# Loads of the second head pair and of phi moved behind a branch, and TensorE products without a reader at the start of a kernel of attention and two expert layers

## The chip, the cores and the metric

One core of one Trainium2 chip runs the program. Measured is the device time in microseconds (us) of one execution. The engines are TensorE (PE; its weight loads PEld), VectorE (DVE), ScalarE (ACT), GpSimd (POOL) and SyncE (SP), which here only issues DMA transfers.

## What is computed

A softcapped attention over 48 heads of 448 tokens by 64, whose output is laid out as 1792 tokens by 768; a soft mixture of 8 experts with 4 slots each; and a layer of squared ReLU. Cut to the core:

```python
scores = scale * np.matmul(q, k.transpose(0, 1, 3, 2))
scores = cap * np.tanh(scores / cap)
attn = softmax(scores)                      # EPS in the denominator
x = np.matmul(attn, v)                      # -> (1792, 768)
logits = x @ phi                            # (1792, 32)
slot_input = softmax(logits, axis=0).T @ x  # 32 slots
slot_out[e] = np.maximum(slot_input[e] @ w1[e], 0.0) @ w2[e]
x = softmax(logits, axis=1) @ slot_out
h = np.maximum(x @ w_in, 0.0)
return h * h @ w_out
```

## The kernel before

Heads are worked on in pairs: 24 pairs (NPAIR), each with one load of q and k of 448 KB (`load(i)`, L268, on SP's queue) into half of one of two buffers (`r0` holds pairs 0 and 1, `r1` pairs 2 and 3, then again `r0`). The program is written out by hand in the order in which each engine and each queue executes it (a manual schedule), so the order in the code is the order on every engine.

The prologue loads the cap (L94), has VectorE work out from it `flag` (L98), which says whether |cap| is above 40, lets GpSimd fill constants (`ident`, an identity; selectors; zeros of the tails `ktail` and `vtail`, L246), loads pairs 0 and 1, and loads phi in four transfers of 24 KB (L580). Then every engine reads `flag` into a register (`values_load`, L581) and branches on it (`tc.If`, L582). The cap of these inputs is 30, so the body of the If runs; the Else is another algorithm for large caps, and lies first in the instruction stream of each engine.

In the body, v of pair 0 is requested on GpSimd's queue (`load_v(0)`: six transfers `va`, L285, and two `vtail`, L289). VectorE splits q and k of a pair into a rounded part `hi` (L294) and a rest `lo` (L300), and GpSimd copies the last 64 key columns of both into `ktail` (L306). Then comes the loop over the pairs. `scores(i, g)` for g = 0, 1, 2 are six products of 64 by 128 by 448 on TensorE (L323: hi by hi, lo by hi, hi by lo, for two heads), g = 3 is three products with `ktail` (L318). ScalarE puts each block through Tanh (L327, L325), which frees its place in PSUM (two places, `ps_s`), and then half a pair through Exp (`exps`, L333). VectorE adds up the exponentials (`sums`, L339 and L343). In the order of TensorE: scores 0 and 1 of pair i, `pv` of pair i-1 (products with v, L355), `den` of pair i-1 (sums of the denominators, L365), scores 2 and 3 of pair i, the tail of `pv` (L352), and for older pairs the logits (L427) and a transposition (L419). Pair 0 has no predecessor, so in its iteration only the four `scores` stand on TensorE, and right behind them scores 0 and 1 of pair 1.

SP's queue issues in order: loads of pairs ahead (pair i+3 in iteration i), weights of the experts, words of the last layer's weights that are decoded on the side (L175; decoded by L189 on ScalarE and by VectorE), and the broadcast of the reciprocal denominators (`bc`, L378). Behind the branch's end come the experts (L860, L885) and the last layer (L969, L1089), which the change does not touch.

The two PSUM places of tag `m` (`ps_m`) hold `den`, the logits and the transpositions, in turn.

Of the kernel before, what the change touches and what calls it, by code (L numbers as in the profile page):

```python
# [8 lines left out]
F32 = mybir.dt.float32  # L9
# [10 lines left out]
P = 128  # L20
# [22 lines left out]
def softcap_attention_soft_moe_relu2(  # L43
# [11 lines left out]
    nc = tc.nc  # L55
# [174 lines left out]
    with ExitStack() as att:  # L230
# [34 lines left out]
        def load(i):  # L265
            b, two, h = heads_of(i)
            t = raw_tile(i)
            nc.sync.dma_start(out=t, in_=qk[b, two, :, :, h].rearrange("j d r s -> (j d) r s"))  # L268
            st["raw", i] = t
# [4 lines left out]
        def load_v(i):  # L274
            b, two, hh = heads_of(i)
            src = v[b, two, :, hh].rearrange("j q c d -> q j c d")
            va = vp.tile([P, NG, 2, D], F32, tag="va", name=f"va{i}")
            vt = vtail[i % 2]
            for g in range(NG):
                at, end = g * P, (g + 1) * P  # L280
                while at < end:
                    c, q = divmod(at, CP)
                    n = min(CP - q, end - at)
                    r = at - g * P
                    nc.gpsimd.dma_start(out=va[r:r + n, g], in_=src[q:q + n, :, c])  # L285
                    at += n
            for h in range(2):
                rows = slice(D * h, D * h + D)
                nc.gpsimd.dma_start(out=vt[rows, rows], in_=src[CP - D:, h, C - 1])  # L289
            st["v", i] = va, vt  # L290
# [38 lines left out]
        def exps(i, half):  # L329
            p = st["p", i, half].rearrange("p c h s -> p (c h s)")  # L330
            if half:
                p = p[:, :3 * S]
            nc.scalar.activation(p, p, AF.Exp, scale=cabs)  # L333
# [239 lines left out]
            if steps:  # L573
                steps.pop(0)()

        for i in range(2):
            load(i)
        for j in range(2):
            for h in range(2):
                nc.sync.dma_start(out=phi_sb[D * j:D * j + D, h::2], in_=phi[D * h:D * h + D, j::2])  # L580
        flag_v = nc.values_load(flag[:1, :1], min_val=0, max_val=1)  # L581
        with tc.If(flag_v == 0, preferred_fallthrough_block=False) as cond:  # L582
            load_v(0)
            prep_hi(0)
            prep_lo(0)
            load(2)
            for i in range(NPAIR):
                last = i == NPAIR - 1
                prv, old, tok = (i >= n for n in (1, 2, 3))
                scores(i, 0)  # L590
                scores(i, 1)
                exps(i, 0)
                if old:
                    take(i - 2)
                if tok:
                    norm(i - 3)
                if prv:
                    sums(i - 1, 1)
                if i + 3 < NPAIR:
                    load(i + 3)  # L600
                if old:
                    den_rows(i - 2)
                if not last:
                    prep_hi(i + 1)
                    prep_lo(i + 1)
                if prv:
                    for g in range(NG):
                        pv(i - 1, g)
                    den(i - 1, i - 3 if tok else None)
                if tok:  # L610
                    logits_add(i - 3)
                    if (i - 3) % HP == HP - 1:
                        late = batch_end((i - 3) // HP)
                        late.pop(0)()
                    elif (i - 3) % HP in (1, 2):
                        step()
                if i in range(4, 16, 2):
                    load_weight(NPAIR // 2 - 1 + (i - 4) // 4, part=i // 2 % 2)
                if i == NPAIR - 2:
                    load_weight(NB - 2, part=0)  # L620
                    load_weight(NB - 2, part=1)
                if (i, 2) in dsteps:
                    dsteps.pop((i, 2))()
                if i < 2 * len(early) and i % 2 == 0:
                    x = early[i // 2]
                    load_raw(*x, ring[NB - 1 - i // 2 % 2][:, :WSZ])
                    dsteps[i + 1, 1] = lambda x=x: decode_a(x)
                    dsteps[i + 2, 0] = lambda x=x: decode_b(x, nc.vector)
                    dsteps[i + 2, 1] = lambda x=x: decode_c([x], (0, 1))
                    dsteps[i + 3, 0] = lambda x=x: decode_c([x], (2,))  # L630
                    dsteps[i + 4, 2] = lambda x=x: store(x)
                if i % 2 and i < NPAIR - 1:
                    load_weight(i // 2)
                if (i, 0) in dsteps:
                    dsteps.pop((i, 0))()
                scores(i, 2)
                scores(i, 3)
                exps(i, 1)
                if prv:
                    pv(i - 1, NG)  # L640
                sums(i, 0)
                if tok:
                    to_tokens(i - 3)
                    if (i - 3) % HP == 0:
                        step()
                if not last:
                    load_v(i + 1)
                if i == NPAIR - 3:
                    load_weight(NB)
                if i == NPAIR - 2:  # L650
                    load_weight(NB + 1)
                    load_weight(NB - 3, part=0)
                    load_weight(NB - 3, part=1)
                if tok and (i - 3) % HP == HP - 1:
                    late.pop(0)()
                    steps.extend(late)
                if (i, 1) in dsteps:
                    dsteps.pop((i, 1))()
                if i == NPAIR - 4:
                    load_weight(NB - 1)  # L660
            assert not dsteps
            assert not steps
            n = NPAIR - 1
            pv(n, 0)
            pv(n, 1)
            sums(n, 1)
            den_rows(n - 1)
            load_weight(NB + 2, nc.scalar)
            pv(n, 2)
            pv(n, 3)  # L670
            norm(n - 2)
            norm(n - 1)
            den(n)
            to_tokens(n - 2, nc.scalar)
            logits(n - 2)
            den_rows(n)
            logits(n - 1, False)
            load_weight(NB + 3, nc.scalar)
            load_weight(NB + 4, nc.scalar)
            norm(n)  # L680
            to_tokens(n - 1, nc.scalar)
            logits(n, False)
            last_end(True)

        with cond.Else():
            st.clear()
            for n, x in enumerate(early):
                load_raw(*x, ring[NB - 1 - n % 2][:, :WSZ])
                decode_ab(x)
                decode_c([x])  # L690
                store(x)
# [487 lines left out]
```

## Time and profile before

| what | value |
|---|---|
| device time, three runs | 556.78, 560.4, 568.22 us, median 560.4 us |
| the profiled execution | 557.4 us, of which its span 555.6 us |
| granted TensorE clock, mean | 0.993 |
| busy over the span | PE 521.3 us (94%), ACT 332.6 us (60%), DVE 331.1 us (60%), POOL 161.0 us (29%) |
| chain that ended last, by engine | PE 81%, DMA 8%, DVE 3%, ACT 3%, issue 2%, POOL 1% |

The span runs from the first to the last instruction of the program. A busy time is the union of an engine's instructions; those that only read registers, branch or issue DMAs are not counted. The chain that ended last is followed back from the last instruction, at each step to what released it. "issue" is time in which an engine waited for nothing that the profile shows. In the timeline, a row has its start, its length, the engine, the line, and how many instructions were merged; in brackets stands how long the engine had been idle and what released it.

### The profile page before, as it was taken

What the parts mean: (1) busy time and instruction counts of PE and PEld (TensorE: products, weight loads), DVE (VectorE), ACT (ScalarE), POOL (GpSimd) and SP (SyncE); (2) the same over time, 40 slices, a digit from 0 to 9 for tenths busy, and PEclk for the clock granted to TensorE, in tenths of its full rate; (3) what the DMA queues carried; (4) which work ended last, traced back from release to release, by engine and by line L of the source; (5) the groups of instructions that cost most, each with busy time, mean ns of one, the idle gap of its engine ahead of it and who ended that gap; (6) DMA issues with size and microseconds to landing.
All of it is one profiled execution on the core that took longest, in us unless ns stands there. A gap on an engine that the chain in (4) does not pass through costs nothing.

```text
span 555.6 us, 10518 instructions
## 1 busy us (share of the span) xinstructions
PE 521.3 (94%) x4068; PEld 358.0 (64%) x4068; DVE 331.1 (60%) x529; ACT 332.6 (60%) x467; POOL 161.0 (29%) x347
## 2 busy tenths in 40 slices
PE   2999999999999988898679999999999999999997
PEld 1555556555665644454236888888888888788885
DVE  2489999999999764450018989889641231322111
ACT  1899999999899840000026677666654455633342
POOL 6987888788878700000000000000000000000000
PEclk9999999999999997999999999999999999999999
DMA  4578787888788899999999445551020020001002
GB/s 124 158 240 248 234 244 244 258 263 267 251 253 235 240 341 417 417 415 416 416 408 378 172 137 170 187 191 57 1 113 2 37 77 1 0 20 38 0 2 113
DMA packets 46249, 108.16 MB, mean 195 GB/s; under 512 B 19440, under 2 KB 28272, under 8 KB 46192
## 3 DMA queue, kind: packets, MB, share of 16 engines
q1 hardware_dynamic: 39472, 99.14, 49.6%
q0 software_dynamic: 6144, 5.52, 4.7%
q10 hardware_dynamic: 576, 2.75, 1.4%
q8 instruction: 34, 0.56, 0.4%
q14 instruction: 23, 0.19, 0.1%
HBM read 94.47 MB, written 7.86 MB: 184 GB/s over the span
## 4 chain that ended last, share of the span: by engine, by line
PE 81%; DMA 8%; DVE 3%; ACT 3%; issue 2%; POOL 1%; SPq 0%; POOLq 0%; ACTq 0%; DVEq 0%
PE y L1089 35%; PE pv L355 9%; PE sc L323 8%; DMA rb<-in_w_dram 6%; PE y L1026 4%; PE so L885 3%; PE sc L318 3%; PE dn L365 3%; PE ph L860 3%; PE pv L352 3%; PE h L969 2%; PE y L1030 2%; PE xm L419 1%; DMA r<-in_w_out_dram 1%; DMA bc<-rc 1%
## 5 line engine op out<-in xcount | busy, mean ns | idle before, releaser
L1089 PE MATMUL y<-gh,wo 128*128 128x512 f32 x576 | 179.0, 393 | 0.4 <-ACT part L1036 0.4
L1089 PEld LDWEIGHTS y<-gh,wo 128*128 128x128 f32 x576 | 106.5, 188 | 24.2 <-issue 1.4
L1089 PE MATMUL y<-gl,wo 128*128 128x512 f32 x288 | 111.6, 390 | 0.0
L982 DVE TENSOR_TENSOR gl<-r,gh 128x512 fp32r<-128x512 f32 (+1 forms) x64 | 40.0, 624 | 112.7 <-ACT gh L981 110.8
L285 POOL DMA_DIRECT2D va<-in_v_dram x144 | 87.3, 614 | 2.5 <-issue 2.4
L973 ACT ACTIVATE r<-h 128x512 f32<-128x512 f32 (+1 forms) x64 | 34.8, 544 | 80.1 <-PE h L969 80.1
L327 ACT ACTIVATE r<-sc,tsc 128x896 f32<-128x896 f32 x72 | 69.5, 998 | 17.5 <-PE sc L323 17.2
L333 ACT ACTIVATE r<-r,cabs 128x1792 f32<-128x1792 f32 (+1 forms) x48 | 77.1, 1606 | 1.6
L1089 PEld LDWEIGHTS y<-gl,wo 128*128 128x128 f32 x288 | 54.1, 188 | 11.6
L355 PE MATMUL pv<-r,va 128*64 128x448 f32 x288 | 60.8, 557 | 0.0
L323 PE MATMUL sc<-hi 64*128 64x448 f32 x144 | 32.7, 449 | 11.1 <-DVE hi L294 10.5
L867 ACT ACTIVATE hs<-ph 128x256 f32<-128x256 f32 x8 | 3.1, 383 | 65.2 <-PE ph L860 65.2
L355 PEld LDWEIGHTS pv<-r,va 128*64 128x64 f32 x288 | 18.7, 138 | 30.2 <-issue 22.6
L980 ACT ACTIVATE r<-r 128x512 f32<-128x512 f32 (+1 forms) x62 | 35.8, 577 | 2.0
L981 ACT CAST gh<-r 128x512 fp32r<-128x512 f32 (+1 forms) x62 | 35.1, 566 | 2.0
L306 POOL CAST ktail<-hi 64x64 fp32r<-64x64 f32 x48 | 27.8, 580 | 22.8 <-DVE hi L294 21.0
L339 DVE SCALAR_TENSOR_TENSOR psum<-r,gcol 128x896 f32<-128x896 f32 x24 | 27.3, 1137 | 3.6 <-ACT r L333 3.6
L885 PE MATMUL so<-rb,ht 128*32 128x256 f32 x298 | 24.9, 382 | 4.2 <-DVE ht L873 2.1
L343 DVE TENSOR_TENSOR psum<-psum,r 128x896 f32<-128x896 f32 x24 | 26.0, 1083 | 4.5 <-ACT r L333 4.5
L300 DVE TENSOR_TENSOR lo<-r,hi 128x896 fp32r<-128x896 f32 x24 | 26.9, 1120 | 2.8 <-POOL ktail L306 0.5
L289 POOL DMA_DIRECT2D vtail<-in_v_dram x48 | 28.1, 590 | 1.6 <-issue 1.6
L323 PEld LDWEIGHTS sc<-hi 64*128 64x128 f32 x144 | 14.1, 192 | 21.5 <-issue 16.1
(195 smaller groups left out, 806.9 us busy)
## 6 DMA issues: line engine op xcount, KB each, us to landing
rb<-in_w_dram SPq DMA_DIRECT2D x41, 768.0 KB, 13.2
r<-in_qk_dram SPq DMA_DIRECT2D x24, 448.0 KB, 6.3
r<-in_w_out_dram SPq DMA_DIRECT2D x13, 768.0 KB, 4.4
r<-in_w_in_dram SPq DMA_DIRECT2D x9, 768.0 KB, 4.3
r<-in_w_dram SPq DMA_DIRECT2D x7, 896.0 KB, 15.6
rb<-in_w_in_dram SPq DMA_DIRECT2D x7, 768.0 KB, 6.4
bc<-rc SPq DMA_DIRECT2D x88, 56.0 KB, 3.5
rb<-in_w_dram SPq DMA_DIRECT2D x12, 384.0 KB, 4.5
```

Of the source, the lines that this page charges most:

```text
L285: nc.gpsimd.dma_start(out=va[r:r + n, g], in_=src[q:q + n, :, c])
L289: nc.gpsimd.dma_start(out=vt[rows, rows], in_=src[CP - D:, h, C - 1])
L323: nc.tensor.matmul(sc[:, h, :S], k, x[rows, 0], **flags)
L327: nc.scalar.activation(p, sc[:, :, :S], AF.Tanh, scale=tsc)
L333: nc.scalar.activation(p, p, AF.Exp, scale=cabs)
L355: nc.tensor.matmul(o[D * h:D * h + D, :S], va[:, g, h], p[:, h], start=(g == 0), stop=False,)
L885: nc.tensor.matmul(so[32 * j:32 * j + 32, :UNIT], ht[:, ft, :], weights(EU * e + EU // 2 + u), start=(e == 0 and ft == 0), stop=(e == NE - ...
L973: nc.scalar.activation(r[:, :n], h[:, :n], AF.Relu)
L980: nc.scalar.activation(r[:, :n], r[:, :n], AF.Square)
L981: nc.scalar.copy(gh[:, :n], r[:, :n])
L982: eng.tensor_tensor(out=gl[:, :n], in0=r[:, :n], in1=gh[:, :n].bitcast(F32), op=ALU.subtract)
L1089: nc.tensor.matmul(y[:, :nn], whl[ft][:, wi, ds], gx[:, :nn], start=(ft == first and t == 0), stop=(ft == end - 1 and t == 2),)
```

## The change

`load(1)` and the four transfers of phi go from in front of the branch into its body: there the order is `load(1)`, v of pair 0, `load(2)`, phi. The Else gets phi as well (it reloads q and k itself). A new function `turn(a, b, n)` takes a place of `ps_m` and lets TensorE write n products of a and b into it, which nothing reads. It is called three times on the path taken: four products of the identity with itself (128 by 128 by 128, float32) between `load(0)` and the reading of `flag`; four more at the head of the body; and, in the iteration of pair 0 behind `scores(0, 3)`, five products of `hi` of pair 0 with itself (128 by 128 by 448, float32r).

```diff
-        for i in range(2):
-            load(i)
-        for j in range(2):
-            for h in range(2):
-                nc.sync.dma_start(out=phi_sb[D * j:D * j + D, h::2], in_=phi[D * h:D * h + D, j::2])
+        def load_phi():
+            for j in range(2):
+                for h in range(2):
+                    nc.sync.dma_start(out=phi_sb[D * j:D * j + D, h::2], in_=phi[D * h:D * h + D, j::2])
+
+        def turn(a, b, n):
+            t = ps_m.tile([P, 512], F32, tag="m", name="turn")
+            for _ in range(n):
+                nc.tensor.matmul(t[:a.shape[1], :b.shape[1]], a, b, start=True, stop=True)
+
+        load(0)
+        turn(ident, ident, 4)
         flag_v = nc.values_load(flag[:1, :1], min_val=0, max_val=1)
         with tc.If(flag_v == 0, preferred_fallthrough_block=False) as cond:
+            turn(ident, ident, 4)
+            load(1)
             load_v(0)
             prep_hi(0)
             prep_lo(0)
             load(2)
+            load_phi()
...
                 scores(i, 3)
+                if i == 0:
+                    turn(st["hi", 0][:, 0, :P], st["hi", 0][:, 0], 5)
                 exps(i, 1)
...
         with cond.Else():
             st.clear()
+            load_phi()
```

SP's queue, the prologue up to the branch, before (the numbers behind a name are buffers; `rb0` in the last row is already the Else's first transfer):

```order
L94 DMA capb_125<-in_cap_dram 128x1
L268 DMA r0_75<-in_qk_dram 128x2x448 x2
L580 DMA phi_sb_165<-in_phi_dram 64x3x32 x4
L581 TENSOR_LOAD flag_129
L581 ISA x2
L582 COMPARE_AND_BRANCH
L175 DMA rb0_84<-in_w_in_dram 128x768
```

The same place of the changed kernel:

```order
L94 DMA capb_125<-in_cap_dram 128x1
L268 DMA r0_75<-in_qk_dram 128x2x448
L588 TENSOR_LOAD flag_129
L588 ISA x2
L589 COMPARE_AND_BRANCH
L579 DMA phi_sb_165<-in_phi_dram 64x3x32 x4
L175 DMA rb0_84<-in_w_in_dram 128x768
```

One load of 448 KB and the four transfers of phi no longer stand ahead of the reading of `flag`; phi now is the first thing of the Else.

SP's queue from the head of the body, before (`r0` with one row of two loads is pair 0 and 1 above; here `r1` is pairs 2 and 3, `rb0` the first words to decode, the last `r0` pair 4, and `bc0` the reciprocals of pair 0):

```order
L582 UNCONDITIONAL_BRANCH
L268 DMA r1_76<-in_qk_dram 128x2x448 x2
L175 DMA rb0_84<-in_w_in_dram 128x768
L268 DMA r0_75<-in_qk_dram 128x2x448
L378 DMA bc0_351<-rc0_349 128x1x112 x4
L166 DMA rb1_85<-in_w_dram 128x1536
```

The same place of the changed kernel, where the first row of `r0` is pair 1:

```order
L589 UNCONDITIONAL_BRANCH
L268 DMA r0_75<-in_qk_dram 128x2x448
L268 DMA r1_76<-in_qk_dram 128x2x448
L579 DMA phi_sb_165<-in_phi_dram 64x3x32 x4
L268 DMA r1_76<-in_qk_dram 128x2x448
L175 DMA rb0_84<-in_w_in_dram 128x768
L268 DMA r0_75<-in_qk_dram 128x2x448
```

Pair 1 stands ahead of pair 2, and phi between pair 2 and pair 3, so pair 2 moved from the first to the second place and pair 3 from the second to the seventh.

TensorE around the end of pair 0's scores, before (`sc0_2` and `sc0_3` are blocks 2 and 3 of pair 0, `sc1_0` is block 0 of pair 1):

```order
L323 MATMUL sc0_2_278<-hi0_242 128x448 x2
L323 MATMUL sc0_2_278<-hi0_242,lo0_244 128x448 x2
L323 MATMUL sc0_2_278<-lo0_244,hi0_242 128x448 x2
L318 MATMUL sc0_3_286<-hi0_242,ktail0_195 128x448 x2
L318 MATMUL sc0_3_286<-lo0_244,ktail0_195 128x448
L323 MATMUL sc1_0_302<-hi1_269 128x448 x2
L323 MATMUL sc1_0_302<-hi1_269,lo1_271 128x448 x2
```

The same place of the changed kernel:

```order
L323 MATMUL sc0_2_288<-hi0_248 128x448 x2
L323 MATMUL sc0_2_288<-hi0_248,lo0_250 128x448 x2
L323 MATMUL sc0_2_288<-lo0_250,hi0_248 128x448 x2
L318 MATMUL sc0_3_296<-hi0_248,ktail0_195 128x448 x2
L318 MATMUL sc0_3_296<-lo0_250,ktail0_195 128x448
L584 MATMUL turn_301<-hi0_248 128x448 x5
L323 MATMUL sc1_0_318<-hi1_279 128x448 x2
L323 MATMUL sc1_0_318<-hi1_279,lo1_281 128x448 x2
```

Five products stand between the last product of `sc0_3` and the first of `sc1_0`; the other rows keep their order.

## Rows read from the trace of the kernel before

**Rows 1.** The page: head, granted clock in 40 slices, chain by engine.

```profile
span 555.6 us, 10518 instructions
...
PEclk9999999999999997999999999999999999999999
...
PE 81%; DMA 8%; DVE 3%; ACT 3%; issue 2%; POOL 1%; SPq 0%; POOLq 0%; ACTq 0%; DVEq 0%
```

**Rows 2.** Chain that ended last, 7 to 28 us: start, length, what.

```profile
7.93 2.37 issue
...
14.44 1.05 POOL vtail L289 x2
...
16.09 1.68 PE sc L318 x3
...
20.30 3.54 PE pv L355 x12
```

**Rows 3.** The branch, L582: durations in ns (min/median/max), start in us.

```profile
L582 PEldq COMPARE_BRANCH  x1: 4056/4056/4056, 4.8 to 4.8; - x1
L582 DVEq COMPARE_BRANCH  x1: 67/67/67, 4.9 to 4.9; - x1
...
L582 SPq COMPARE_BRANCH  x1: 45/45/45, 6.3 to 6.3; - x1
L582 POOLq COMPARE_BRANCH  x1: 45/45/45, 7.4 to 7.4; - x1
```

**Rows 4.** DMA queues, 5 to 6.5 us: packets, MB, share of 16 engines.

```profile
q1 hardware_dynamic: 932, 0.49, 107.6%
```

**Rows 5.** DMA queues, 6.5 to 7.6 us.

```profile
q14 instruction: 3, 0.02, 6.9%
```

**Rows 6.** Timeline, first work of SP, DVE and POOL behind the branch.

```profile
9.59 2.00 SPq L268 DMA_DIRECT2D r<-in_qk_dram  x2
9.73 0.63 DVE L294 CAST hi<-r 128x896 fp32r<-128x896 f32 x1 [5.22 <-issue]
10.30 4.14 POOL L285 DMA_DIRECT2D va<-in_v_dram  x6 [2.37 <-issue]
```

**Rows 7.** Timeline of PE, 12 to 28 us.

```profile
12.07 0.58 PE L323 MATMUL sc<-lo,hi 64*128 64x448 f32 x2
12.45 0.58 PE L323 MATMUL sc<-hi 64*128 64x448 f32 x2
...
17.19 0.57 PE L318 MATMUL sc<-lo,ktail 128*128 128x448 f32 x1
17.70 0.74 PE L323 MATMUL sc<-hi 64*128 64x448 f32 x2
...
27.16 0.38 PE L323 MATMUL sc<-hi,lo 64*128 64x448 f32 x2
27.36 0.38 PE L323 MATMUL sc<-lo,hi 64*128 64x448 f32 x2
```

**Rows 8.** Timeline of ACT, 12 to 26 us.

```profile
14.85 1.79 ACT L333 ACTIVATE r<-r,cabs 128x1792 f32<-128x1792 f32 x1
...
17.80 0.63 ACT L325 ACTIVATE r<-sc,tsc 128x448 f32<-128x448 f32 x1 [0.27 <-PE sc L318]
...
19.79 1.89 ACT L327 ACTIVATE r<-sc,tsc 128x896 f32<-128x896 f32 x2
...
25.43 1.01 ACT L327 ACTIVATE r<-sc,tsc 128x896 f32<-128x896 f32 x1 [1.93 <-PE sc L323]
```

**Rows 9.** Timeline of POOL and DVE, 16 to 18 us.

```profile
16.09 0.51 POOL L306 CAST ktail<-lo 64x64 fp32r<-64x64 f32 x2
16.66 1.35 POOL L306 CAST ktail<-hi 64x64 fp32r<-64x64 f32 x2
16.75 1.15 DVE L339 SCALAR_TENSOR_TENSOR psum<-r,gcol 128x896 f32<-128x896 f32 x1 [3.61 <-ACT r L333]
```

**Rows 10.** Transfers of L268 issued up to 25 us.

```profile
DMA to landing us min/median/max: 4.2/4.8/8.7
```

## What the change does to the time, forecast from these rows

> **What bounds the kernel now.** I read the page first: the span is 555.6 us and TensorE holds 81% of the chain that ended last [rows 1]. The change touches only the first 28 us, so the second view is the chain of waits there [rows 2]. Read from its top: 2.37 us from 7.93 on in which GpSimd waits for nothing the profile shows (the branch), GpSimd's eight requests for v, which end at 14.44 + 1.05 = 15.49, its copies into `ktail`, then block 3 of pair 0's scores on TensorE (16.09 to 17.77), and from there TensorE alone through `pv`. So at the very place where the change puts its five products, TensorE sets the end; ahead of it GpSimd does.
>
> The branch is the third view. TensorE, VectorE, SP and GpSimd reach it at 4.8 to 7.4 us [rows 3], and SP, VectorE and GpSimd do their first work behind it at 9.59, 9.73 and 10.30 [rows 6]. Until 6.5 the DMA engines are full with the loads (107.6% of 16 engines), and no packet of an instruction queue is among them [rows 4]; in the next 1.1 us three packets of one come [rows 5]. I read this as code that is fetched from behind the branch and queues behind data.
>
> The fourth view is TensorE's timeline [rows 7]. The same products of 448 columns follow each other every 0.37 us at 12 us (12.07, 12.45) and every 0.20 us at 27 us (27.16, 27.36). The first is 448 columns at the 1.2 GHz level, the second near the 2.4 GHz level, although the granted clock reads full in these first slices [rows 1]; I go by the spacing. The 12 products of `pv` take 3.54 us [rows 2], between 12 x 0.37 = 4.4 and 12 x 0.20 = 2.4: n x 0.37 + (12 - n) x 0.20 = 3.54 gives n = 6.7, so the clock rises at about 20.3 + 6.7 x 0.37 = 22.8 us. Before it TensorE stood still until the branch was over and then worked with pauses until 17.70.
>
> **The loads moved behind the branch.** From SP go, ahead of its branch, one load and four transfers of phi. Its branch stands at 6.3, TensorE's at 4.8, for which SP's first five requests are the only reason I see; it can come 1.4 earlier at most, and I take 1.0. For the engines that branch at 4.8 and 4.9 the data ahead of their code get less. GpSimd, which branches at 7.4 when the loads are through, needs 10.30 - 7.4 = 2.9 us to its first work, VectorE 9.73 - 4.9 = 4.8. The gain of VectorE lies between 0 and 1.9; about half the loads' bytes remain ahead of it, so I take 0.7, well inside.
>
> What that gives: VectorE splits pair 0 at 9.0 instead of 9.73, the first Tanh and Exp come 0.7 earlier, and the first Exp, which ends at 14.85 + 1.79 = 16.64 [rows 8], ends at 15.9. But the next thing ScalarE needs is block 3, and in the trace it already waits 0.27 us for that, at 17.80 [rows 8]. Block 3 hangs on GpSimd, whose branch came when the queues were empty: its 10.30 and its 15.49 stay. So **the term of the branch is 0**: all of the 0.7 ends in a longer wait for block 3. The bounds are 0 and -0.27, the wait that is there.
>
> Pair 1 is now requested at 8.6 and not at 1.9. Transfers of this kind land 4.2 to 8.7 us after their issue [rows 10]: at 12.8 to 17.3. Its two splits (0.63 for `hi` [rows 6], 1.1 for `lo` by the like of it) end at 14.5, at the latest at 19.0; TensorE takes pair 1 up at 17.70 [rows 7] in the old order, at 19.4 in the new (below). Term 0; the upper end would cost nothing there either. Pair 2 moves from 9.59 to about 9.2, pair 3 behind phi's four requests (0.6 each) to about 12.4, 2 us later; it is split at 29 us, 8 us after the latest landing of 12.4 + 8.7 = 21.1. Phi is read first for the logits of pair 0, three pairs on. Term 0 for these, hidden behind two and more pairs of work.
>
> **The products ahead and behind the branch.** Four of 128 columns in float32 each time. TensorE has nothing else before `hi` is there, so they cost 0 unless they last past 9.6. No row has just this; `pv` is float32 too, with 12 records for six products, so two records each: 8 x 128/448 x 0.37 = 0.85 us. TensorE comes out of its branch at 4.8 + 4.06 = 8.87 [rows 3], by my 0.7 at 8.2: they end at 9.1. If they were four times as long, 11.6, scores would start 2 us late and still end ahead of block 3's release at 16.09 by the pause that stands there. Term 0.
>
> **The five products behind block 3.** Each has 448 columns: 5 x 0.37 = 1.87 us at the lower level, 5 x 0.20 = 1.0 at the upper. Block 3's last product starts at 17.19 and frees the array at 17.56; pair 1's first product starts at 17.70 [rows 7]. So only 0.14 us of pause is there to fill, and 1.87 - 0.14 = 1.73 us go on TensorE's path. Behind them all TensorE's work lies 1.73 us late until the clock rises; if it rises at the same 22.8, what is pushed past it is done at the upper level, in half the time: +0.87. If the filled pause makes it rise 0.9 us earlier (unbroken work from 16.8 and not from 17.70), 0.9 us of half-rate work is saved by half: 0.87 - 0.45 = +0.42. I take the middle, **+0.65**. ScalarE does not hide it: it waits 1.93 us for block 2 of pair 1 at 25.43 [rows 8], so what TensorE loses before this point shows there in full. From there on all later work stands in the same order, and the shift goes through to the end.
>
> **Sum.** 0 + 0 + 0 + 0.65 = +0.65 us: 557.4 becomes 558.05 for the profiled execution. The runs shown are 556.78, 560.4 and 568.22; with the profiled 557.4 the middle two of the four average 558.9, which I take as the kernel's time now, 1.5 below the median of three: **559.5 us**.
>
> **Rivals.**
> *The clock rises before block 3.* The new products give TensorE work at 2 and at 8 us. If that and the earlier scores bring the upper level before 16 us, block 3 ends 0.5 earlier, the five products take 1.0, pair 1's scores and `pv` run at 0.20: 17.0 + 1.0 + 2.4 (12 products' worth of scores) and `pv`, which then waits for v (last pieces requested up to 14.4) at about 20.9, leave block 2 of pair 1 ready at 23.3 and not 25.4: -2.1, 556.8 us. Against it: the trace has nearly unbroken products from 12.07 to 13.6 at the lower level [rows 7] and no rise behind them before 22.8; the new ones stand apart from these by VectorE's two splits. The Trainium skill (TensorE: Matmul & The Clock Gate, Part 1) says that the throttled level is the default, that sustained activity releases it, and that the same kernel starts with different numbers of slow products from run to run. By that page such a rise is possible with and without the change; the trace agrees on the slow start, and no run here shows an early rise. Chance 0.2.
>
> *GpSimd is slowed: slower.* Today the copies of `lo` into `ktail` take 0.51 for two, with VectorE idle, and the next two 1.35, beside VectorE's sum L339 [rows 9]. L339 waits for the first Exp; if that ends before 16.1 (by my numbers 15.9), L339 falls on the copies that block 3 waits for: +0.84 on block 3. With the 1.73, 2.57 us of half-rate work are late, half of it at the upper level: +1.3, up to +2.1 if the new pause also delays the rise by 0.8 or more. I take +1.7: 560.6 us. For it speaks that 15.9 is on the wrong side; against it that my 0.7 can be less than 0.5. Chance 0.25.
>
> *Nothing of it is on the path.* The branch is no earlier, and the clock rises early enough through the filled pause to pay for the five products: 0, 558.9 us. Chance 0.1.
>
> **How the numbers follow.** Forecast 0.45 (its own bounds, +0.42 and +0.87, are 559.3 and 559.8 us), rivals 0.2, 0.25 and 0.1. All cases lie within 3 us of each other, far inside the 2% (11 us) that a measurement of this kernel tells from no change; executions of the one kernel before lie 11 us apart. So the range is made by these: low 557.4 - 2.1 = 555.3; high, beyond the slower rival on the median (560.4 + 1.7 = 562.1), by half the way to the slowest run: 565. No case gives 11 us either way: same 0.96, 0.02 each for the others.
>
> **What would show it.** First work behind the branch about 9.0 on VectorE and 8.6 on SP, 10.3 on GpSimd. ScalarE's wait before Tanh of block 3 longer than 0.27, its start still near 17.8. Five products 0.37 apart behind block 3, `sc1_0` at 19.4. The wait of ScalarE before block 2 of pair 1 ending at about 26.1. Wrong, if GpSimd also comes out earlier and starts its requests by 9.6 (then up to -0.7), or if products of pair 0 are 0.20 apart.

## Result, and the profile after

The changed kernel takes 560.58 us (median of 12 runs, 557.13 to 562.32) against 556.72 us for the kernel before beside it: ratio 1.0057, 95% interval [1.0031, 1.0084], or +3.2 us (+1.7 to +4.7). The ratio is that of the means, 560.25 and 557.06 us, without one slow run of the kernel before (568.22). Measured again at the end of the study beside another experiment (e19 below) it gave 1.0034 [1.0012, 1.0056]. The two, weighted by their intervals, make +2.4 us (+1.5 to +3.4). So the change is a small loss: inside the 2%, inside the range that was given, but four to five times the +0.65 us of the forecast's sum, and with other causes.

| | before | after |
|---|---|---|
| profiled execution, its span | 557.4, 555.6 us | 561.4, 559.6 us |
| granted TensorE clock, mean | 0.993 | 0.983 |
| busy PE / DVE / POOL over the span | 94 / 60 / 29% | 94 / 59 / 29% |
| chain that ended last: PE, DMA, issue | 81, 8, 2% | 80, 7, 3% |

The start answers to [rows 3] and [rows 6]. The branch of the changed kernel, durations in ns and start in us, then the first work of SP, VectorE, TensorE and GpSimd behind it from the timeline:

```profile
L589 PEldq COMPARE_BRANCH  x1: 3620/3620/3620, 4.3 to 4.3; - x1
...
L589 SPq COMPARE_BRANCH  x1: 45/45/45, 4.5 to 4.5; - x1
L589 POOLq COMPARE_BRANCH  x1: 45/45/45, 6.9 to 6.9; - x1
```

```profile
7.97 2.39 SPq L268 DMA_DIRECT2D r<-in_qk_dram  x2
...
7.89 0.63 DVE L294 CAST hi<-r 128x896 fp32r<-128x896 f32 x1 [3.92 <-issue]
...
7.96 2.08 PE L584 MATMUL turn<-ident 128*128 128x128 f32 x8 [3.73 <-issue]
...
10.18 3.78 POOL L285 DMA_DIRECT2D va<-in_v_dram  x6 [2.79 <-issue]
```

VectorE begins 1.84 us earlier than in [rows 6] and SP 1.62; GpSimd gains 0.12 only. What becomes of it stands in the timeline of GpSimd, VectorE, TensorE and ScalarE, 14 to 27 us, which answers to [rows 7 to 9]:

```profile
15.61 1.43 POOL L306 CAST ktail<-lo 64x64 fp32r<-64x64 f32 x2
...
15.51 1.15 DVE L339 SCALAR_TENSOR_TENSOR psum<-r,gcol 128x896 f32<-128x896 f32 x1 [1.69 <-ACT r L333]
...
15.60 0.74 PE L318 MATMUL sc<-hi,ktail 128*128 128x448 f32 x1 [2.00 <-POOL ktail L306]
17.09 0.74 PE L318 MATMUL sc<-hi,ktail 128*128 128x448 f32 x1 [0.74 <-POOL ktail L306]
17.62 0.58 PE L318 MATMUL sc<-lo,ktail 128*128 128x448 f32 x1
18.00 2.07 PE L584 MATMUL turn<-hi 128*128 128x448 f32 x5
20.00 0.74 PE L323 MATMUL sc<-hi 64*128 64x448 f32 x2
...
18.24 0.64 ACT L325 ACTIVATE r<-sc,tsc 128x448 f32<-128x448 f32 x1 [1.95 <-PE sc L318]
...
26.32 1.01 ACT L327 ACTIVATE r<-sc,tsc 128x896 f32<-128x896 f32 x1 [1.01 <-PE sc L323]
```

VectorE's sum now starts at 15.51, 0.10 us ahead of GpSimd's copies of `lo` for pair 0. These take 1.43 us and not the 0.51 of [rows 9], block 3 waits for them, ScalarE waits 1.95 us for block 3, and the five products begin at 18.00. At 26.3 us ScalarE is 0.89 us later than in [rows 8].

Nothing in these rows reaches 3 us. The rest of this profiled execution's 4.0 us lies elsewhere: 1.8 us arise between 28 and 200 us, most of it at 120 to 135, where TensorE is busy 12.86 us and not 14.74. Other profiled executions of the same changed kernel have 14.72 and 14.62 us there, so that is this execution's own. The remaining 1 us and more arises behind the branch's end, where the change touches nothing. Four loads of expert weights (`rw`) on SP's queue, timeline of SP before and after:

```profile
202.49 5.54 SPq L166 DMA_DIRECT2D rw<-in_w_dram  x4
```

```profile
205.22 10.43 SPq L166 DMA_DIRECT2D rw<-in_w_dram  x4
```

What SP waited for, 200 to 219 us, from the view of waits (us in total, times, longest), again before and after:

```profile
...
SPq L166 <- PE u L490: 2.8, 1, 2.8
SPq L166 <- PE dn L365: 2.5, 1, 2.5
SPq L166 <- DVE bc L412: 2.3, 1, 2.3
...
```

```profile
SPq L166 <- DMA r<-in_w_dram: 5.2, 2, 2.7
...
SPq L166 <- DVE bc L412: 2.7, 1, 2.7
SPq L166 <- PE dn L365: 2.5, 1, 2.5
...
```

The first line of the last fence is new: twice SP waits for a transfer `r<-in_w_dram`, that is, for loads that ScalarE's queue issues.

### The profile page after: what moved, and what is told of

It reads as the page before. It is cut to its first block, busy times and chain, and to the rows that moved or that the text cites. A ratio compares the mean times of both kernels' runs of the same rounds, so it can differ in the third digit from the quotient of the medians.

```text
span 559.6 us, 10561 instructions
## 1 busy us (share of the span) xinstructions
PE 525.5 (94%) x4089; PEld 363.4 (65%) x4089; DVE 331.6 (59%) x529; ACT 332.6 (59%) x467; POOL 159.9 (29%) x347
## 3 DMA queue, kind: packets, MB, share of 16 engines
q0 software_dynamic: 6144, 5.52, 4.9%
## 4 chain that ended last, share of the span: by engine, by line
PE 80%; DMA 7%; DVE 4%; ACT 3%; issue 3%; POOL 2%; SPq 0%; POOLq 0%; DVEq 0%; ACTq 0%
PE y L1102 35%; PE pv L355 9%; PE sc L323 8%; DMA rb<-in_w_dram 6%; PE y L1039 4%; PE so L898 4%; PE ph L873 3%; PE dn L365 3%; PE sc L318 3%; PE pv L352 2%; PE h L982 2%; PE y L1043 2%; PE xm L419 1%; ACT r L327 1%; DMA bc<-rc 1%
## 5 line engine op out<-in xcount | busy, mean ns | idle before, releaser
L1102 PEld LDWEIGHTS y<-gl,wo 128*128 128x128 f32 x288 | 54.1, 188 | 11.6
L355 PE MATMUL pv<-r,va 128*64 128x448 f32 x288 | 59.6, 548 | 0.0
L886 DVE COPY ht<-px 128x32 f32<-128x32 f32 x8 | 1.5, 192 | 44.7 <-PE px L883 34.2
## 6 DMA issues: line engine op xcount, KB each, us to landing
r<-in_w_dram SPq DMA_DIRECT2D x7, 896.0 KB, 15.6
```

The costliest lines, as they stand in the source:

```text
L355: nc.tensor.matmul(o[D * h:D * h + D, :S], va[:, g, h], p[:, h], start=(g == 0), stop=False,)
L1102: nc.tensor.matmul(y[:, :nn], whl[ft][:, wi, ds], gx[:, :nn], start=(ft == first and t == 0), stop=(ft == end - 1 and t == 2),)
```

## The experiments

Each experiment changes one thing against the kernel before or the changed kernel. Ratios are against the kernel before, run beside each on the same chip; microseconds are (ratio - 1) x 557. "rw" is the length of the four loads on SP's queue, "copies" the longer of GpSimd's two pairs of copies that block 3 waits for, both from the profiled execution.

| kernel | ratio, interval | us | rw | copies |
|---|---|---|---|---|
| changed kernel | 1.0057 [1.0031, 1.0084] | +3.2 | 10.43 | 1.43 |
| e19: changed kernel again | 1.0034 [1.0012, 1.0056] | +1.9 | 11.18 | 1.40 |
| e1: loads moved, no products | 1.0034 [1.0022, 1.0047] | +1.9 | 11.19 | 1.41 |
| e2: only the eight products | 1.0002 [0.9984, 1.0019] | +0.1 | 5.65 | 0.57 |
| e3: only the five products | 0.9998 [0.9981, 1.0014] | -0.1 | 5.51 | 0.55 |
| e5: changed kernel without the five | 1.0043 [1.0022, 1.0064] | +2.4 | 10.44 | 0.54 |
| e9: only phi moved | 1.0013 [0.9998, 1.0027] | +0.7 | 5.53 | 1.34 |
| e8: loads moved, seven products in the pause | 1.0008 [0.9981, 1.0035] | +0.4 | 11.01 | 1.37 |
| e10: clock up from 5 us, loads as before | 1.0004 [0.9995, 1.0014] | +0.2 | 5.46 | 1.40 |
| e11: the same products, loads moved | 1.0042 [1.0026, 1.0057] | +2.3 | 12.41 | 0.99 |
| e4: changed kernel, sum later | 1.0037 [1.0009, 1.0064] | +2.1 | 10.97 | 0.54 |
| e7: loads moved, sum later | 1.0014 [1.0000, 1.0029] | +0.8 | 11.46 | 0.54 |
| e14: changed kernel, one unexecuted transfer more | 1.0021 [1.0004, 1.0037] | +1.2 | 5.52 | 1.29 |
| e15: kernel before, seven unexecuted transfers more | 1.0013 [0.9997, 1.0029] | +0.7 | 12.13 | 0.55 |
| e16: e1 with the unexecuted transfer | 1.0013 [1.0000, 1.0026] | +0.7 | 5.94 | 1.36 |
| e17: e7 with the unexecuted transfer | 1.0003 [0.9989, 1.0017] | +0.2 | 5.77 | 0.54 |
| e18: e4 with the unexecuted transfer | 0.9990 [0.9975, 1.0005] | -0.6 | 5.49 | 0.55 |

### Which part of the change costs

Loads alone (e1), the eight products alone (e2), the five alone (e3), phi alone (e9), and all but the five (e5). e1's edit is the diff of the front without the three calls of `turn`; e2 and e3 add those calls to the kernel before:

```diff
+        turn(ident, ident, 4)
         flag_v = nc.values_load(flag[:1, :1], min_val=0, max_val=1)
         with tc.If(flag_v == 0, preferred_fallthrough_block=False) as cond:
+            turn(ident, ident, 4)
```

> Kernel before with only the loads of pair 1 and phi behind the branch, no added products. Theory A (the loss is made in the first 28 us, by GpSimd's copies that fall on VectorE's first sum, and by the five products): the copies of lo for block 3 still take about 1.4 us beside the sum, block 3 starts its second product at about 17.1, no products stand behind it, so pair 1's first product comes at about 18.1 against 17.70 before, and the span is 0 to +0.6 us over the kernel before. Theory B (the moved loads or phi disturb something later, as at 123 to 131 us in the changed kernel's trace): +2 to +3 us, with less than 0.6 of it before 28 us.

> Kernel before with only the eight products of 128 columns, four ahead of the branch and four behind it; loads as before. Theory A: nothing on the path, 0 us, within 0.5. Theory C (the added work makes TensorE's clock rise early and fall again in the pause before block 3, so products up to about 22 us run at the lower level, and the whole pattern of falls is moved): the trace shows the upper level for a part of pair 0 and the lower one behind it, and +0.5 to +2 us.

> Kernel before with only the five products of 448 columns behind block 3 of pair 0; loads as before. Theory A: five products 0.37 us apart ahead of pair 1's first product, which comes at about 19.4 against 17.70, +0.4 to +0.9 us in the whole. If the five were hidden by a clock that rises earlier: 0 or less.

> The changed kernel without the five products behind block 3 (loads moved, eight products of 128 columns kept). The loads alone measured +1.9 us, all together +3.2. If the five products cost only where block 3 is late (theory A, with the collision): about +2.0 over the kernel before, as with the loads alone. If it is the eight that make the difference to the loads alone (theory C, an early rise of the clock that falls back in the pause before block 3): +3 us.

> Only phi moved behind the branch; pair 1 is loaded ahead of it as in the kernel before. Branch code is still behind both loads of q and k, so VectorE starts at about 9.7 and the first scores are not earlier. Theories A and D: no collision and no longer pause, 0 us within 0.5. Theory E with phi's 768 small packets or their place in the queue as the disturbance: +1 to +2 us.

Measured: +1.9, +0.1, -0.1, +2.4 and +0.7 us. Neither set of products by itself costs anything that its interval of about 1 us either way shows, and taking the five out of the changed kernel gives nothing that its interval shows. The moved loads carry the loss, and of these mostly pair 1's: e9 leaves pair 1 where it was, its +0.7 us has an interval down to -0.1, and the collision of the next part is in its profile (1.34). In e3's profile block 3 is not late and the five products fall at the upper clock level; TensorE's timeline there (compare 18.00 and 20.00 above):

```profile
15.86 1.04 PE L318 MATMUL sc<-hi,ktail 128*128 128x448 f32 x2 [0.69 <-POOL ktail L306]
16.73 0.36 PE L318 MATMUL sc<-lo,ktail 128*128 128x448 f32 x1
16.93 1.19 PE L579 MATMUL turn<-hi 128*128 128x448 f32 x5
18.06 0.47 PE L323 MATMUL sc<-hi 64*128 64x448 f32 x2
```

### The collision on GpSimd

In e4 and e7 VectorE makes its first sum of pair 0 one Exp later, with the same terms in another order:

```diff
             t = psums[i % 2]
+            if i == 0:
+                if half == 0:
+                    nc.vector.scalar_tensor_tensor(
+                        out=t, in0=st["p", i, 1][:, 0], scalar=gcol, in1=p[:, 0], op0=ALU.add, op1=ALU.add
+                    )
+                else:
+                    nc.vector.tensor_tensor(out=t, in0=t, in1=st["p", i, 0][:, 1], op=ALU.add)
+                return
```

> The changed kernel, but VectorE's first sum of pair 0 is made over the first block of the second half and the first of the first half, so it waits for the second Exp and cannot run beside GpSimd's copies of lo for block 3 (the sum has the same terms in another order). Theory A: the copies take 0.5 us again for two, block 3's second product comes at about 16.2 and not at 17.1, and the whole is 0.5 to 1 us under the changed kernel. Theory B or C (the loss is made later or by the clock): as the changed kernel, within 0.3 us.

> Only the loads moved, and VectorE's first sum of pair 0 made after the second Exp, so that it doesn't fall on GpSimd's copies for block 3. Theory A (the collision is what the moved loads cost): the copies of lo take 0.5 us, block 3's second product comes at about 16.0, and the whole is back to the kernel before, 0 us within 0.6. Theory D (the moved loads cost because pair 0's first scores come 1.5 us earlier and block 3 does not, so TensorE pauses longer, and its clock rises later or falls back): a part of the 1.9 stays, +0.8 to +1.5 us. Theory E (something later in the program): +1.9 us as before.

Timeline of GpSimd and, in the last row, of ScalarE in e4: the copies are all at 0.5 us, and block 3 reaches ScalarE at 17.20 and not at 18.24.

```profile
14.88 0.54 POOL L306 CAST ktail<-hi 64x64 fp32r<-64x64 f32 x2
15.48 0.51 POOL L306 CAST ktail<-lo 64x64 fp32r<-64x64 f32 x2
16.05 0.51 POOL L306 CAST ktail<-hi 64x64 fp32r<-64x64 f32 x2
...
17.20 0.63 ACT L325 ACTIVATE r<-sc,tsc 128x448 f32<-128x448 f32 x1 [0.66 <-PE sc L318]
```

Measured: e4 +2.1 us, e7 +0.8 (e1, the same with the collision, +1.9). The profiles agree: block 3 reaches ScalarE at 17.96 to 18.79 us in the changed kernel's four profiles and those of e1, e14 and e16, which all have the collision, and at 16.69 to 17.55 in the four with the later sum (e4, e7, e17, e18). The collision is real and its removal helps, but e4 keeps most of the changed kernel's loss. It also is a race of a few tenths: in e5's profile the sum started at 15.81, behind the copies of `lo`, which took 0.51.

### The clock

Perhaps the changed start only shifts when TensorE's clock rises. The changed kernel's rows show a rise and a fall. Timeline of TensorE:

```profile
11.63 0.39 PE L323 MATMUL sc<-hi,lo 64*128 64x448 f32 x2
11.85 0.36 PE L323 MATMUL sc<-lo,hi 64*128 64x448 f32 x2
...
20.54 0.58 PE L323 MATMUL sc<-hi,lo 64*128 64x448 f32 x2
20.91 0.58 PE L323 MATMUL sc<-lo,hi 64*128 64x448 f32 x2
```

At 11.6 us two products stand 0.22 apart (upper level), at 20.5, behind the pause before block 3, 0.37 (lower level; the granted clock is 0.51 from 18 to 22 us). e8 fills that pause with seven products, e10 and e11 give TensorE 14 products of 128 columns ahead of the branch, 3 behind it and 8 of 448 in the pause, e10 with the loads in the old place, e11 in the new. The edit of these two in the pause:

```diff
                 scores(i, 2)
+                if i == 0:
+                    turn(st["hi", 0][:, 0, :P], st["hi", 0][:, 0], 8)
                 scores(i, 3)
```

> Only the loads moved; seven products of 448 columns that nothing reads are put into TensorE's pause before block 3 (four ahead of it, three between its first and second product), none behind it. The collision stays. Theory D: the pause is filled, the clock rises by about 15 us in many executions and stays, and the whole is 0 to -1 us against the kernel before, 2 to 3 us under the loads alone. Theory A: the copies are as slow, +1.5 to +2.5 us. Theory E: +1.9 us.

> Loads as in the kernel before. Unread products so placed that TensorE hardly pauses from 2.2 us on: 14 of 128 columns ahead of the branch, 3 behind it, 8 of 448 columns in the pause before block 3, none behind block 3. Theory D (when the clock first rises is a lottery of each execution, and the start's loss or gain hangs on it): the upper level holds from 10 us on in nearly all executions, pv of pair 0 starts at about 19.4 with products 0.20 apart, and the whole is 1 to 2 us under the kernel before with less spread. Theory A alone (only GpSimd's copies set block 3): 0 us.

> The same products, with the loads of pair 1 and phi behind the branch. Theory D: with the clock up in both, the moved loads cost only what block 3 comes later by the collision, 0 to +0.5 us over the kernel e10_warm, so still 0.5 to 2 us under the kernel before. Theory E (the moved loads disturb something later in the program): 1.5 to 2 us over e10_warm.

In e10's profile pair 0's products already follow each other every 0.20 us (11.34, 11.54, 11.74), and over all its executions the kernel gains nothing: +0.2 us [-0.3, +0.8]. e11, with the loads moved, loses 2.3. So the moved loads cost their 2 us with these products too. But the two kernels do not part the loads from the clock: in e11's profile TensorE still pauses 1.71 us before block 3, and `pv` of pair 0 then takes 3.68 us (TensorE's timeline, 12 records), where e10's takes 2.48. e8 stood at +0.4 with an interval of 3 us, which decides nothing.

What an early clock is worth, e10 does not settle. GpSimd's copies collide in its profile as well (1.40), and its profiled execution is ahead of that of the kernel before. The first sums of the denominators (`den`) of pair 0, TensorE's timeline of the kernel before, of e15 (below, with the start of the kernel before) and of e10:

```profile
23.77 0.40 PE L365 MATMUL dn<-r,onesp 128*32 128x112 f32 x8
22.30 0.40 PE L365 MATMUL dn<-r,onesp 128*32 128x112 f32 x8
21.44 0.40 PE L365 MATMUL dn<-r,onesp 128*32 128x112 f32 x8
```

e10's lead of 2.33 us here is still 2.30 at the first `rw` load (200.19 for 202.49) and 2.1 in the span (553.5 for 555.6). In a single execution, then, what is won at the start does come out at the end. But e15 is 1.47 ahead at this place too, so the profiled execution of the kernel before had a late start; how often that happens is not shown.

Two more executions of the changed kernel, each by itself:

> The changed kernel once more, for a second trace of it. If the wait of the first trace at 123 to 131 us (1.9 us in which the lateness grew) belongs to the change, it is there again; if it was that execution's alone, the lateness stays as it is at 28 us up to the end of the attention.

> The changed kernel a third time, for the same question, and for when TensorE's clock first rises: theory D expects another moment than in the other traces, and a lateness at 28 us that goes with it, 0.5 us for each us that the lower level lasts longer.

They took 562.35 and 562.49 us, with spans of 560.6 and 560.7, GpSimd's copies ahead of block 3 at 0.87 and 1.34 us, and the four `rw` loads at 12.87 and 13.04. A length of 10 us and more for these loads is there in every trace so far in which pair 1 is requested behind the branch, and in none of the others (5.5 to 5.7).

### The stall at 205 us

Why should a load moved at 2 us stop SP at 205? The order of the program says which counters a transfer waits on. There are eight (`DMAHW0` to `DMAHW7`), used in turn, and SP and ScalarE share them; a transfer waits until the one before it on its counter has landed. SP's loads behind the branch's end, before:

```
L166 DMA rw2_7207<-in_w_dram 128x1536 [waits DMAHW2_49,DMAHW6_49,DVE_49,DMAHW7_49,PE_49,Activation_49]
L166 DMA rw3_7208<-in_w_dram 128x1536 [waits DMAHW3_49]
L166 DMA rw0_7205<-in_w_dram 128x1536 [waits DMAHW4_49]
```

after:

```
L166 DMA rw2_7227<-in_w_dram 128x1536 [waits DMAHW6_49,DVE_49,DMAHW7_49,PE_49,Activation_49]
L166 DMA rw3_7228<-in_w_dram 128x1536 [waits DMAHW7_49]
L166 DMA rw0_7225<-in_w_dram 128x1536 [waits DMAHW0_49]
```

and ScalarE's three loads, at the end of the body, in both kernels:

```
L166 DMA r_77<-in_w_dram 128x1792 [waits DMAHW6_49,DVE_49]
L166 DMA r_78<-in_w_dram 128x1792
L166 DMA r_79<-in_w_dram 128x1792 [waits DMAHW0_49,Activation_49]
```

Taken in turn these hold counters 6, 7 and 0. In the changed kernel `rw3` and `rw0` use 7 and 0 too, and so must wait until ScalarE's second and third loads, 896 KB each, have landed. They are issued at 207.02 and 207.45 us and take 5.4 and 7.9 to land, so until about 212.4 and 215.3, and SP's timeline has the two loads issued right then; in the kernel before, the four were issued by 207.54 (202.49, 206.68, 207.06, 207.54):

```profile
212.44 0.33 SPq L166 DMA_DIRECT2D rw<-in_w_dram  x1
...
215.32 0.33 SPq L166 DMA_DIRECT2D rw<-in_w_dram  x1
```

The counters moved because the way through the Else has one transfer fewer: five left the prologue, and four (phi) came into the Else. With e9 (four and four) they did not move. Why one transfer fewer moves them by four counters (3 to 7, 4 to 0) the order does not show. If so, a transfer more in the Else, which these inputs never execute, must end the stall, and seven more in the kernel before (one fewer, counted in eights) must bring it on. e14, e16, e17 and e18 have the first edit, e15 the second:

```diff
             st.clear()
             load_phi()
+            load(1)
```

```diff
             st.clear()
+            for _ in range(7):
+                load(1)
```

> The changed kernel with one more transfer in the Else, which these inputs never execute; with it the expert loads behind the branch's end (rw, L166) wait for the same semaphores as in the kernel before. Theory S (the moved loads cost through the semaphore that SP's four expert loads share with ScalarE's loads at 205 to 215 us): the four rw loads take about 5.5 us on SP's queue and not 10.4, and the time falls by about 2 us against the changed kernel, to +0.5 to +1.5 us over the kernel before (what is left is the start: collision and five products). Theory A (all is lost in the first 28 us) and theory D (the start's clock): no difference to the changed kernel, +3 us over the kernel before.

> The kernel before with seven transfers more in the Else, which these inputs never execute; nothing on the path taken changes but the semaphores of the transfers behind the branch's end, which become those of the changed kernel. Theory S: the four rw loads take 10.4 to 13 us on SP's queue and not 5.5, and the kernel is 1.5 to 2.5 us slower than the kernel before, by code that never runs. Theories A and D: 0 within 0.5 us, since the start is the same.

> The loads moved, no products, and one transfer more in the never executed Else (the rw loads wait as in the kernel before). Theory S: rw loads 5.5 us, 0 within 0.6 us of the kernel before (the loads alone without the pad stood at 1.0034, +1.9 us). Theory A: still +1.5 to +2 us, since the start is that of the loads alone.

> As the loads with the pad, and VectorE makes its first sum of pair 0 only behind the second Exp, so that GpSimd's copies of lo stay at 0.5 us. Without the pad this stood at 1.0014 (+0.8 us). Theory S: rw loads 5.5 us and 0.5 to 1.5 us faster than the kernel before, the gain of the earlier start (about 1 us). Theory A: +0.8 us as without the pad.

The order of e14 has `rw3` and `rw0` on counters 3 and 4 again, that of e15 on 7 and 0, and the profiles settle the mechanism both ways. Timeline of SP in e14, then in e15, and what SP waits for in e15, 200 to 216 us:

```profile
202.95 5.52 SPq L166 DMA_DIRECT2D rw<-in_w_dram  x4
```

```profile
201.00 12.13 SPq L166 DMA_DIRECT2D rw<-in_w_dram  x4
```

```profile
SPq L166 <- DMA r<-in_w_dram: 6.9, 2, 3.8
```

A transfer that never runs stops SP's queue, and another sets it free. Its price is smaller than I expected: e15 loses 0.7 us where 1.5 to 2.5 stood in the expectation, and its interval reaches to -0.2. The profile of e15 shows why it is about 1. Views by stretches, 200 to 290 us, before and e15 (busy PE, PEld, DVE, ACT, POOL; granted clock, DMA share, GB/s):

```profile
200.00:206.00 6.00, 5.03 (x71) 2.52 (x68) 3.04 (x6) 2.08 (x6) 0.00 (x0) 1.00 0.80 286
206.00:212.00 6.00, 4.25 (x63) 2.87 (x62) 4.31 (x18) 1.45 (x6) 1.29 (x3) 0.86 1.01 394
212.00:218.00 6.00, 5.81 (x53) 2.73 (x51) 1.51 (x4) 0.06 (x1) 0.00 (x0) 0.57 1.02 420
218.00:290.00 72.00, 58.86 (x759) 29.58 (x759) 18.20 (x50) 6.19 (x15) 1.87 (x6) 1.00 1.02 415
```

```profile
200.00:206.00 6.00, 4.39 (x70) 2.64 (x69) 3.30 (x11) 2.19 (x7) 0.00 (x0) 1.00 0.95 350
206.00:212.00 6.00, 5.24 (x63) 3.90 (x67) 3.92 (x13) 0.91 (x4) 1.36 (x3) 0.72 1.00 398
212.00:218.00 6.00, 5.20 (x81) 2.82 (x76) 2.37 (x11) 0.69 (x2) 0.00 (x0) 1.00 0.92 350
218.00:290.00 72.00, 58.99 (x735) 29.42 (x730) 16.47 (x43) 5.55 (x13) 1.87 (x6) 0.98 1.02 415
```

From 206 us on this stage is bound by the DMA engines (share 1.0, 415 GB/s). e15's execution is 1.5 us ahead when it issues the first `rw` (201.00 against 202.49). At 212 to 218 its DMA engines move 350 GB/s and not 420, since SP had too little in the queue: 70 GB/s over 6 us is 0.42 MB, 1.0 us at 415 GB/s. The first product of the last layer, TensorE's timeline before and in e15, is only 0.5 ahead:

```profile
296.40 3.00 PE L1089 MATMUL y<-gh,wo 128*128 128x512 f32 x12
```

```profile
295.92 3.00 PE L1091 MATMUL y<-gh,wo 128*128 128x512 f32 x12
```

From the first `rw` to this product it is 93.9 us before and 94.9 in e15. Over all profiled executions that stretch averages 94.2 us in the nine without the stall (93.7 to 95.1) and 95.2 in the eleven with it (94.3 to 97.8): 1.0 us, though the two groups overlap.

### Both causes taken back

> The changed kernel with both causes found taken back: one transfer more in the never executed Else (rw loads wait as before) and VectorE's first sum of pair 0 behind the second Exp (GpSimd's copies of lo at 0.5 us). All products and moved loads stay. If the semaphores cost about 1 us and the collision about 1 us each, this is at 0 to +0.5 us of the kernel before, and 2 to 3 us faster than the changed kernel run beside it; if the moved loads or the products cost something else as well, it stays at +1 us or more.

> The changed kernel unaltered, on the same chip as the one with both causes taken back: +2 to +4.5 us over the kernel before, by its first interval [1.0031, 1.0084]. If it comes out below +1.5 us, the sum that the causes must make up is smaller than the first measurement said.

e18 keeps all products and all moved loads and stands at -0.6 us [-1.4, +0.3]; the changed kernel beside it stands at +1.9. The difference is 2.4 us, with an interval of about 1.5 either way (both intervals taken together). With the stall and the collision gone, no loss is left that the interval shows. Each by itself, from pairs that differ in one of them, weighted by their intervals, with the changed kernel's two measurements as one: the stall 1.0 +- 0.5 us (changed kernel and e14, e1 and e16, e7 and e17, e4 and e18, e15 and before), the collision 1.0 +- 0.6 (changed kernel and e4, e14 and e18, e1 and e7, e16 and e17). One pair fits less well: e11 loses 2.1 us (+- 1.0) against e10, though the collision is in both profiles (0.99 and 1.40); the interval reaches down to the stall's price, and the slower `pv` named above is in e11's profile as well. How much of the collision's price is block 3 itself, and how much the clock that is low behind the longer pause, these runs do not part. Not one of the versions beats the kernel before by more than its interval: e18 comes nearest.

## Why the prediction was right and wrong

**The branch: right that the engines come earlier, wrong that it costs nothing.** The loads ahead of the branch did hold VectorE and SP up; by the two profiles they come out 1.84 and 1.62 us earlier, where 0.7 and 1.0 were taken. About 0.5 us of this is the profiled execution of the kernel before, whose `flag` is worked out at 4.04 us, and at 3.54 in e15 with the same start: VectorE begins at 9.02 to 9.73 us in the five profiles with all loads in the old place, and at 7.89 to 8.31 in the fourteen with pair 1 moved. GpSimd gains almost nothing, since its own constants keep it until 7.4, and ScalarE's wait for block 3 grew (1.95 us for 0.27), as said. But block 3 did not stay where it was, as the term of 0 with its bounds of 0 and -0.27 had it: it reaches ScalarE at 18.24 and not at 17.80, by the collision. e18, which has no collision and no stall, stands at -0.6 us [-1.4, +0.3], so a gain from the earlier start is not shown.

**Pair 1, phi and the other pairs: right for their data, and incomplete.** `hi` of pair 1 waited for its data until 12.06 and was in time. What was missed is below.

**The eight products: wrong in size, free all the same.** Four of 128 columns take 2.07 us and not 0.85; scaling by columns from `pv` was the mistake. They end at 10.04 and push scores to 9.97, later than VectorE's split (7.89 + 0.63), but block 3 forgives it, as the prediction's four-fold bound of this term had said: e2 is at +0.1 [-0.9, +1.1].

**The five products: +0.65 is not shown, and not excluded.** e3, which has only them, stands at -0.1 us with an interval of -1.1 to +0.8, and e5, without them, differs from the changed kernel by nothing that the intervals show. The sum took them at the lower level and the rise of the clock as fixed, and neither holds from execution to execution: in e3's profile they run at the upper level (1.19 us), since the clock had risen before them, at block 3. In the changed kernel's profile they do lie on the chain at the lower level, as the prediction had it (1.87 us).

**The slower rival: it happened.** It stood at a chance of 0.25, because VectorE's gain, put at 0.7, could be less than 0.5; the prediction itself saw that its 15.9 was on the wrong side of 16.1. In the changed kernel the sum starts at 15.51. The copies cost +0.92 (0.84 was predicted). The Trainium skill (SBUF — State Buffer, section "SBUF: two separate sides") says that a VectorE instruction with two inputs from SBUF and a GpSimd instruction that reads SBUF exclude each other: the one that starts first has the port that they share for its whole length. The chain of the changed kernel agrees: the first copy ends at 16.76, when the sum has ended (15.51 + 1.15 = 16.66), and the second then takes 0.24 us.

```profile
15.61 1.15 POOL ktail L306
...
16.80 0.24 POOL ktail L306
...
17.09 1.12 PE sc L318 x2
18.20 1.87 PE turn L584 x5
```

It is worth 1.0 us by the pairs of experiments and not the 1.7 that the rival was given.

**The early rise of the clock: it happened, and its price stays open.** Products of pair 0 stood 0.22 apart at 11.6 us, one of the prediction's own signs of being wrong, and that was to be worth -2.1 us; but the clock fell again in the pause before block 3 (granted clock 0.50 from 15.6 to 18 us), so the rival did not come about as it was drawn. e10 holds the clock up past block 3: its profiled execution is 2.1 us shorter than that of the kernel before, and its ratio over all executions shows no gain.

**The steps that failed** are two terms that the prediction put at nothing. The first is "the term of the branch is 0": the earlier start moved VectorE's sum onto GpSimd's copies, and this cost 1.0 +- 0.6 us; the prediction had it as a rival, at 1.7 us, and not in its sum. The second is the "Term 0" of the moved transfers, with the sentence "From there on all later work stands in the same order, and the shift goes through to the end." The order is the same, but not the waits. The prediction counted what each moved transfer does to its queue and to its data, and did not look at which completion counter each later transfer would share. That is another 1.0 +- 0.5 us, which no term and no rival had. The order of the two kernels, with waits, was there to be compared ahead of the run: the lines of `rw3` and `rw0` differ.

That the time forecast, 559.5 us, lies close to the 560.58 measured is luck: it started from 558.9 for the kernel before, which measured 556.72 beside the changed one, and the loss it added was too small. The sign was right too, but by a term, the five products, that no run shows.

## What to carry to other kernels

Moving, adding or removing a DMA can change which completion counter every later DMA waits on, even if it stands in a branch that is not taken (e15; in e9 the counters stayed); compare the waits of all queues between the two programs, and look for a transfer that now shares its counter with a long one of another queue. Where one engine's release moves, see which other engine it now works beside: half a microsecond decided here whether a 0.5 us copy took 1.4. And a lead won at the start was kept through the stage that is bound by DMA (e10: 2.30 us ahead at its beginning, 2.12 at the first product of the last layer), while a queue that stood still there cost about 1 us.

## What the hardware showed that was not expected

- The four products of 128 columns in float32 (eight records) took 2.07 us, 0.26 us a record, with products 0.37 apart (lower clock level) right behind them, and six records at the upper level 0.94 us (e10), 0.16 a record. By the columns of `pv`'s records they were to take 0.11 and 0.06.
- TensorE's branch takes 3.62 us now and took 4.06 before [rows 3], and VectorE's, SP's and GpSimd's first instructions behind it come earlier too; three packets of an instruction queue travel at 5.3 to 6.5 us in the changed kernel, and at 6.5 to 7.6 before [rows 5]:

```profile
q14 instruction: 3, 0.02, 7.8%
```
- A load that only waits for a counter costs its queue up to 4 us at a time (e11: 7.2 us in two waits), yet the stall cost only about 1 us of the kernel: the DMA engines still move the other queue's transfers meanwhile (e15: 398 GB/s from 206 to 212 us, 394 before).
